# One attention-plus-FFN layer on one core: the 64-row remainders of the first FFN matrix as pairs on the two row halves, its bias in the evictions, and the first chunk's projection in six pieces

## The chip, the cores and the metric

The kernel runs on one core of a Trainium2 chip. The metric is the device time of one execution in microseconds (us). A profiled execution has a span, from its first to its last instruction, and the time of the whole execution, which is a little longer.

## What is computed

One layer over 2048 tokens of width 576, all in bf16: a memory-augmented attention with 32 heads of 18, and a dense FFN of width 4608. `B_x` is not used: the FFN's input is the attention's output.

```python
def _A_ref(x, wq, wk, wv, wo, beta):
    q, k, v = ...                       # (B, H, N=4 segments, L=512, Dh=18)
    phi = lambda t: jnp.where(t > 0, t + 1.0, jnp.exp(t))
    g = _sigmoid(beta).reshape(1, H, 1, 1)
    ...
    for s in range(N):
        logits = jnp.einsum('bhqd,bhkd->bhqk', qs, ks) * scale + mask   # causal, inside the segment
        a_dot = jnp.einsum('bhqk,bhkd->bhqd', _softmax(logits, axis=-1), vs)
        a_mem = einsum(phi(qs), M) / (einsum(phi(qs), z) + 1e-06)
        outs.append(g * a_mem + (1.0 - g) * a_dot)
        M = M + einsum(phi(ks), vs)
        z = z + sum(phi(ks))
    return o @ wo

def _B_ref(x, w1, b1, w2, b2):
    h = _gelu(jnp.einsum('bsd,df->bsf', x, w1) + b1)
    return jnp.einsum('bsf,fd->bsd', h, w2) + b2

h = x + _A_ref(_layernorm(x), A_wq, A_wk, A_wv, A_wo, A_beta)
out = h + _B_ref(_layernorm(h), B_w1, B_b1, B_w2, B_b2)
```

## The kernel before

**Tiling.** The tokens are cut into 8 chunks of 256 (`NCH`, `Q`), each of two tiles of 128 rows (`tl`). The width 576 is contracted in five steps: four of 128 rows and a remainder of 64. In the kernel before, the remainder is 65 rows (`KTAIL`): row 65 of the moving operand holds ones, and row 65 of the weights holds a bias or zeros. The helper `mm5` (lines 321 to 324) issues the four full steps on line 323 and the 65-row step on line 324.

**Streams.** TensorE's work is written as generators, one for each part:
- `stream_P(tl)`: layernorm, the transposed input (`xT`), the projection to q, k and v (three times 576 columns, for every chunk in four pieces of 432, `CH`), its evictions into `qk_pad` and `v_aug`, and the transposes of q and k into `QT` and `KT`: on TensorE for the first two chunks (`TP`), by DMA for the others.
- `stream_A`: 80 visits. A visit is 16 score matmuls on 32-row tiles (line 512), into the four PSUM banks `st4`, an exponential over all four banks on ScalarE (line 518), masks on GpSimd (line 522), and 16 matmuls with the values into the bank `ox` (line 541).
- `stream_M`: the memory's sums; `stream_B(tl)`: the output projection, the residual, the second layernorm, and the transposed FFN input `xn2T`.
- `stream_F1`: the first FFN matrix. Its weights come in 9 groups of 512 columns for every chunk (`w1g`, two buffers, and three more inside `hT` for the first chunk). A unit is two blocks of 128 hidden units by 256 tokens, into one bank: 2 x 5 matmuls, then one eviction on VectorE (line 756) into `hT`. The bias is the 65th row of the weights. For the first chunk the first five groups (`AHEAD`) are run for each 128-token tile apart (line 733). GELU runs in place on `hT` (line 764).
- `stream_F2`: the second matrix, 36 matmuls of 288 columns into one bank (line 790), and the addition of the stored `hc` (line 794).

**PSUM.** Four banks are the scores' (`st4`). Three banks, and `ox` before the first and after the last score visit, are handed out by `bank_slots`. `f_slots` is the same object as `bank_slots`.

**Order.** The kernel plans itself before it issues anything. Every operation is recorded with an engine, an estimated duration, what it reads and writes, and a due time (`SLACK` by kind). `step` walks a simulated clock: on each engine the ready operation with the earliest due time begins; on TensorE the next stream in a fixed order (FFN first or last, by `lead` and `balance`) that is ready and has a free bank. All is then issued in the planned order, so each engine's order on the chip is fixed, and only the semaphores decide when an instruction starts. Where no stream is ready in the beginning, the plan puts in dummy matmuls (line 831).

Of the kernel before, what the change touches and what calls it, by code (L numbers as in the profile page):

```python
# [16 lines left out]
def kernel(  # L17
# [31 lines left out]
    XW = 640  # L49
    CH = 432  # L50
# [7 lines left out]
    def sbuf(name, shape, dt=BF16):  # L58
# [10 lines left out]
    SLACK = dict(head=34, lnp=34, lnb=20.5, pow=-97, apply=-7, ek_k=91, relu_k=47.5, min_k=4, add_k=59, mz=27, exp=21,  # L69
                 ek=-56, relu=43, min=76, add=-35.5, hb=-169.5, gelu=-80, finish=2.5, mem=-93, sum=-137.5, out=-24.5,  # L70
                 hd=133.5, xp=-183.5, xb=-26, t_x=-46.5, t_q=-17.5, t_k=61.5, t_o=-59, t_h=77, w1=29, w2=117, hc=15.5,
                 evict=9, qk=-57.5, ot=-2, mask=32.5, lead=1.5, balance=58.5)
    ops = []
    now, dma_free, table = 0.0, 0.0, "exp"
    free_at = {"PE": 0.0, "SP": 0.0, "ACT": 0.0, "DVE": 0.0, "POOL": 0.0}
    port_until = {"DVE": 0.0, "POOL": 0.0}
    queue = {e: [] for e in free_at}
    writer, readers, known = {}, {}, {}

    class Op:  # L80
        start, end, at, apart = None, NEVER, None, False
# [6 lines left out]
        def ready(self):  # L88
            if self.at is None:
                t = latest(self.preds, self.eng)  # L90
                if t >= NEVER:
                    return NEVER
                self.at = t
            return self.at
# [29 lines left out]
    def op(eng, dur, issue, rd=(), wr=(), slack=0.0, table=None, port=None):  # L124
        o = Op(eng, dur, issue, preds_of(rd, wr), now + slack, table)
        o.port = eng == "POOL" if port is None else port
        ops.append(o)
        queue[eng].append(o)
        note(o, rd, wr)
        return o  # L130
# [8 lines left out]
    def dma(kb, issue, rd=(), wr=(), slack=0.0):  # L139
        return transfer(op("SP", 0.46, issue, rd, wr, slack), kb, 1.66, rd, wr)  # L140
# [6 lines left out]
    def begin(o):  # L147
        nonlocal dma_free, table
# [4 lines left out]
        if getattr(o, "port", False):  # L153
            dur += max(0.0, port_until["POOL" if o.eng == "DVE" else "DVE"] - now)
            port_until[o.eng] = now + dur
        if o.eng == "SP":
            dur = max(dur, dma_free - now - 6.0)
        o.start, o.end = now, now + dur
# [4 lines left out]
        elif d:  # L163
            dma_free = max(dma_free, o.end - o.dur + d.first) + d.dur / DMA_RATE
            d.start, d.end = o.start, dma_free + 0.9
        queue[o.eng].remove(o)

    class Slots:
# [13 lines left out]
        def when(self):  # L182
            return min((self.at(k) for k in self.free), default=NEVER)
# [15 lines left out]
    w1_bufs = [sbuf(f"w1g{j}", [KT, 512]) for j in range(2)]  # L199
    ident = sbuf("ident", [P])  # L200
    mhalf = sbuf("mhalf", [1], F32)
# [39 lines left out]
    LATER, AHEAD = 0, 5  # L241
    f_slots = bank_slots
# [7 lines left out]
    b1_row = B_b1.rearrange("(o f) -> o f", o=1)  # L250
# [8 lines left out]
    def memset(eng, dur, ap, value, key, slack=0.0):  # L259
        e = nc.vector if eng == "DVE" else nc.gpsimd  # L260
        op(eng, dur, lambda: e.memset(ap, value), (), [key], slack)
# [9 lines left out]
    def constants():  # L271
        op("POOL", 0.75, lambda: make_identity(nc, ident[:]), (), ["ident"])
# [11 lines left out]
        for tl in range(2):  # L284
            layernorm(f"p{tl}", x_p[tl][:], ("x_p", tl), xn1[tl], ("xn1", tl), False, -5)
# [5 lines left out]
        for j in range(2):  # L291
            memset("POOL", 0.45, phik_pads[j][:, :, Dh:32], 0.0, ("phik", j, "pad"), slack=5)
        for j in range(2):
            memset("POOL", 0.2, o_nats[j][:, :, D:XW], 0.0, ("o", j, "pad"), slack=6)
            memset("POOL", 0.15, xn2[j][:, D:XW], 0.0, ("xn2", j, "pad"), slack=6)
# [585 lines left out]
```

## Time and profile before

| | |
|---|---|
| time, median of 3 runs | 481.13 us (479.82 to 482.57) |
| the profiled execution's own time | 484.58 us |
| its span | 482.9 us |
| mean granted TensorE clock | 0.992 |
| busy share of the span: TensorE, VectorE, ScalarE, GpSimd | 98%, 58%, 60%, 43% |
| TensorE matmuls | 6084 |

In the profile, PE is TensorE's matmuls, PEld its weight loads, DVE VectorE, ACT ScalarE, POOL GpSimd, SP the engine that issues the DMAs. A matmul's shown duration reaches from its start to its modelled end; matmuls in a row overlap, so the slot that one takes is read from the starts. In a timeline row the columns are start, duration (both us), engine, line, operation, tiles, rows x columns of the array, shape, and the count of merged instructions; brackets hold the idle time before it and what ended that.

### The profile page before, as it was taken

The numbers are of one execution on the slowest core, as the hardware profiler recorded it, in microseconds if no ns is written. First come the engines' busy times: TensorE is split into PE (matmuls) and PEld (weight loads), VectorE is DVE, ScalarE is ACT, GpSimd is POOL, SyncE is SP. The second block draws the span as 40 slices with busy tenths as digits, with TensorE's granted clock in tenths as the row PEclk, the third lists the DMA queues.
The fourth block names the chain that finished last, engine by engine and source line by source line (L and its number), as shares of the span: only waits on it lengthen the run. The fifth ranks groups of instructions, "written<-read, shape, count | busy, mean of one in ns | idle before, by whom it ended". The sixth has DMA issues, their size and how long they took to land.

```text
span 482.9 us, 14420 instructions
## 1 busy us (share of the span) xinstructions
PE 471.1 (98%) x6084; PEld 369.5 (77%) x6084; DVE 282.4 (58%) x688; ACT 289.9 (60%) x206; POOL 207.2 (43%) x291
## 2 busy tenths in 40 slices
PE   7989899999999999999999999999999999999997
PEld 5667778768678878767788888778787788888875
DVE  5787776768676563667685546756555345334401
ACT  2669578971695877951687868475587762213200
POOL 5558355475736342684654343845534511000000
PEclk9989899999999999999999999999999999999999
DMA  7985679779788547668967569693667267646311
GB/s 215 293 280 187 125 128 252 162 144 177 152 169 213 172 118 205 177 121 198 214 136 190 123 165 203 158 233 104 155 196 186 78 190 195 185 124 186 97 50 50
DMA packets 117345, 80.97 MB, mean 168 GB/s; under 512 B 56392, under 2 KB 115232, under 8 KB 117280
## 3 DMA queue, kind: packets, MB, share of 16 engines
q1 hardware_dynamic: 117248, 80.04, 68.0%
q8 instruction: 48, 0.79, 0.7%
q14 instruction: 17, 0.14, 0.1%
q0 software_dynamic: 32, 0.01, 0.1%
HBM read 60.10 MB, written 7.08 MB: 139 GB/s over the span
## 4 chain that ended last, share of the span: by engine, by line
PE 89%; DMA 4%; DVE 3%; issue 1%; POOL 1%; SPq 1%; ACT 1%; DVEq 0%; POOLq 0%
PE bank L323 38%; PE bank L790 23%; PE bank L324 9%; PE ox L541 6%; PE st L512 5%; PE ox L790 4%; DMA wqkv<-in_A_wv_dram 2%; DMA w1g<-in_B_w_dram 1%; PE ox L323 1%; DMA xT<-o_nat 1%; PE bank L564 1%; PE bank L470 1%; PE bank L431 1%; DVE gmzm L311 1%; ACT pt L518 0%
## 5 line engine op out<-in xcount | busy, mean ns | idle before, releaser
L518 ACT ACTIVATE pt<-st 128x2048 bf16<-128x2048 f32 x80 | 150.2, 1877 | 67.1 <-PE st L512 63.7
L323 PE MATMUL bank<-xn2T,w1g 128*128 128x256 bf16 (+1 forms) x1064 | 147.9, 269 | 0.5 <-DVE hT L736 0.3
L790 PE MATMUL bank<-w_sb,hT 128*128 128x288 bf16 x1008 | 138.3, 286 | 0.0
L756 DVE CAST hT<-bank 128x512 bf16<-128x512 f32 x129 | 88.7, 689 | 73.6 <-PE bank L324 72.5
L790 PEld LDWEIGHTS <-hT 128*128 128x128 bf16 x1152 | 109.3, 98 | 28.0
L522 POOL TENSOR_SCALAR_AFFINE_SELECT pt<-pt 128x512 bf16<-128x512 bf16 x128 | 81.0, 648 | 101.6 <-ACT pt L518 101.1
L323 PEld LDWEIGHTS <-w1g 128*128 128x128 bf16 x1104 | 101.0, 97 | 16.8 <-DMA w1g<-in_B_w_dram 0.5
L764 ACT ACTIVATE hT<-hT 128x4608 bf16<-128x4608 bf16 (+4 forms) x23 | 66.1, 2875 | 49.5 <-DVE hT L756 49.4
L324 PE MATMUL bank<-xn2T,w1g 65*128 65x256 bf16 (+1 forms) x266 | 72.1, 271 | 0.0
L323 PE MATMUL bank<-wqkv,xT 128*128 128x432 bf16 x252 | 56.4, 346 | 0.7 <-DMA xT<-xn 0.4
L323 PEld LDWEIGHTS <-xT 128*128 128x128 bf16 x384 | 35.0, 98 | 23.5 <-issue 2.3
L541 PEld LDWEIGHTS <-pt 128*128 128x128 bf16 x1280 | 43.4, 96 | 8.2 <-issue 2.1
L541 PE MATMUL ox<-v_aug,pt 128*128 128x19 bf16 x1280 | 45.8, 172 | 2.0 <-issue 2.0
L512 PE MATMUL st<-QT,KT 32*128 32x128 bf16 x1280 | 32.4, 218 | 0.1
L556 POOL TENSOR_TENSOR pq<-ek,pq 128x512 bf16<-128x512 bf16 x24 | 27.7, 1153 | 6.9 <-DVE ek L554 6.5
L406 ACT CAST qk_pad<-bank 128x432 bf16<-128x432 f32 x31 | 15.8, 522 | 24.7 <-PE bank L324 21.8
L794 DVE TENSOR_TENSOR ot<-bank,hc 128x288 bf16<-128x288 f32 x28 | 12.7, 454 | 28.6 <-PE bank L790 28.1
L512 PEld LDWEIGHTS <-KT 32*128 32x128 bf16 x1280 | 18.7, 93 | 14.0 <-issue 11.7
L324 PEld LDWEIGHTS <-w1g 65*128 65x128 bf16 x276 | 26.8, 97 | 3.2
L586 POOL TENSOR_TENSOR o_nat<-t,t 128x288 bf16<-128x288 f32 x24 | 19.5, 811 | 12.0 <-DVE t L585 11.9
L677 POOL TENSOR_TENSOR h_t<-h_t,b_bc 128x576 f32<-128x576 f32 x16 | 20.6, 1286 | 5.6 <-DVE xn L343 5.6
L324 PE MATMUL bank<-wqkv,xT 65*128 65x432 bf16 x63 | 21.9, 348 | 0.0
(101 smaller groups left out, 484.7 us busy)
## 6 DMA issues: line engine op xcount, KB each, us to landing
w1g<-in_B_w_dram SPq DMA_DIRECT2D x67, 512.0 KB
w_sb<-in_B_w_dram SPq DMA_DIRECT2D x6, 864.0 KB
hd<-h_t SPq DMA_DIRECT2D x16, 288.0 KB
hc<-hd SPq DMA_DIRECT2D x32, 144.0 KB
w1g<-in_B_w_dram SPq DMA_DIRECT2D x67, 64.0 KB
x_b<-in_A_x_dram SPq DMA_DIRECT2D x18, 144.0 KB
hT<-in_B_w_dram SPq DMA_DIRECT2D x5, 512.0 KB
out_dram<-ot SPq DMA_DIRECT2D x16, 144.0 KB
```

Source lines behind the costliest of these rows:

```text
L323: nc.tensor.matmul(out=out_ap, lhsT=lhsT_of(slice(0, P), k), rhs=rhs_of(slice(0, P), k), start=(k == 0), stop=False)
L324: nc.tensor.matmul(out=out_ap, lhsT=lhsT_of(slice(0, KTAIL), 4), rhs=rhs_of(slice(0, KTAIL), 4), start=False, stop=True)
L512: nc.tensor.matmul(out=st4[:, i, n * P:(n + 1) * P], lhsT=KTs[(c - c % 2 + kt // 2) % 3][rows, g, (kt % 2) * P:(kt % 2 + 1) * P], rhs=QTs[ ...
L518: op("ACT", 1.88, lambda: nc.scalar.activation(out=pt[:], in_=st4[:], func=ACT.Exp, scale=scale), sk, [("pt", slot, n) for n in range(4)], ...
L522: op("POOL", 0.65, lambda n=n: nc.gpsimd.affine_select(out=pt[:, :, n * P:(n + 1) * P], in_=pt[:, :, n * P:(n + 1) * P], pattern=[[0, 4], ...
L541: nc.tensor.matmul(out=oxv[:, 4 * (g % 4) + i, :], lhsT=pts[slot][:, i, n * P:(n + 1) * P], rhs=v_augs[(2 * s0 + kt) % 6][:, 4 * g + i, :] ...
L556: op("POOL", 1.16, lambda: nc.gpsimd.tensor_tensor(out=pq[:], in0=e_g, in1=pq[:], op=ALU.add), ["ek"], ["pq"], slack=SLACK["add"])
L586: op("POOL", 0.8, lambda: nc.gpsimd.tensor_tensor(out=o_dst, in0=t1[:], in1=t2[:], op=ALU.add), ["t1", "t2"], ok, slack=SLACK["sum"])
L677: op("POOL", 1.36, lambda: nc.gpsimd.tensor_tensor(out=h_t[:], in0=h_t[:], in1=b2_bc[:], op=ALU.add), ["b2"], [("h", tl)], slack=SLACK["hb"])
L756: op("DVE", 0.684, lambda hT=hT, jp=jp, acc=acc: nc.vector.tensor_copy(out=hT[:, 2 * jp:2 * jp + 2, :], in_=acc), [b], [("hT", c % 2, jp)] ...
L764: op("ACT", (f1 - f0) * Q * 0.00083 + 0.18, lambda hT=hT, f0=f0, f1=f1: nc.scalar.activation(out=hT[:, f0:f1, :], in_=hT[:, f0:f1, :], fun ...
L790: nc.tensor.matmul(out=acc, lhsT=hT[:, q, tl * P:(tl + 1) * P], rhs=w2_sb[:, q, hs], start=(q == 0), stop=(q == NF - 1))
```

## The change

**Remainders.** From the sixth group of the first chunk on, a weight group's bank pair is opened by four 64-row matmuls, two on the upper and two on the lower row half of the array, and the sixteen full steps follow. For this the remainder of the weights is stored as 64 rows by 256 columns on partitions 0 to 63 and again 256 columns on partitions 64 to 127, and `xn2` is written with its last 64 columns twice, so that its transpose has the remainder on both row halves. A group takes two banks at once. For the first five groups of the first chunk the remainder runs as a full step of 128 rows against `xz`, which is zero on the other half.

**Bias.** `b1` is loaded once as 36 rows, transposed on TensorE into `b1T`, and added in the eviction: on VectorE as an addition with a broadcast operand, or on ScalarE as two activations with a bias. The planner takes the engine that is free first (`either`); the same choice is given to the copies of the projection and of the transposes.

**First chunk.** Its projection is cut in six pieces of 288 columns (`NS`); the transposes of q and of k follow directly on their two pieces, and the scores may start before v is projected (`half_V`).

**Planner.** It knows a cost for a change of the tiling (`SWITCH`), chooses the order of remainders and scores by it, models TensorE's code fetch and the port that VectorE and GpSimd share otherwise, holds GpSimd's early memsets by `hold`, and has other durations and other values of `SLACK`. The scores' four banks are used by the scores alone, as before; `f_slots` is gone.

```diff
+    W1 = 4 * 512 + 256
...
-    SLACK = dict(head=34, lnp=34, lnb=20.5, pow=-97, apply=-7, ...
+    SLACK = dict(head=61, lnp=21.5, lnb=50, pow=-21, apply=-5.5, ...
+                 out=-29.5, ..., alone=-163, linger=128.6,
+                 x1=151.5, hold=-1, ln0=86.5)
...
+    def either(first, second, rd, wr, slack=0.0):
+        o = op(*first, rd, wr, slack)
+        o.ways = {eng: (dur, issue) for eng, dur, issue in (first, second)}
+        queue[second[0]].append(o)
+        return o
...
+        if o.eng == "PE" and o.mode != tiling:
+            dur += SWITCH
+            tiling = o.mode
...
-    f_slots = bank_slots
...
     for tl in range(2):
-        load_x(2 + tl, x_b[tl], ("x_b", tl))
+        load_x(2 + tl, x_b[tl], ("x_b", tl), SLACK["x1"])
...
+        memset("POOL", 0.3, xz[:], 0.0, "xz0", slack=6, hold=SLACK["hold"])
...
+        def apply():
+            for to, f0, f1 in ((0, 0, D), (D, 512, D))[0:2 if f32 else 1]:
+                nc.vector.tensor_scalar(out=dst[:, to:to + f1 - f0], in0=src[:, f0:f1], scalar1=mv[:, 0:1], scalar2=rstd[:],
+                                        op0=ALU.subtract, op1=ALU.mult)
...
+            cuts = [(n, n + HALF) for n in range(0, 3 * D, HALF)] if c < NS else [(n, n + CH) for n in range(0, 3 * D, CH)]
...
+            def move(dst, src, n, key):
+                either(("ACT", n * 0.00083 + 0.16, lambda: nc.scalar.copy(out=dst, in_=src)),
+                       ("DVE", n * 0.00104 + 0.16, lambda: nc.vector.tensor_copy(out=dst, in_=src)), [b], [key])
...
+                    yield need(lambda: all(kt in half_V for kt in key_tiles(c, {kt for _, kt in units})), None,
+                               [("pt", slot, n) for n in part] + value_keys(c, units), ["ox"])
...
-        dma(64, lambda: nc.sync.dma_start(out=wt[0:64, 4, :], in_=B_w1[512:576, fcols]), (), [k + ("t",)], SLACK["w1"])
-        dma(1, lambda: nc.sync.dma_start(out=wt[64:KTAIL, 4, :], in_=b1_row[:, fcols]), (), [k + ("b",)], SLACK["w1"])
+        for h in range(2):
+            f0 = fg * 512 + h * Q
+            dma(45, lambda h=h, f0=f0: nc.sync.dma_start(out=wt[64 * h:64 * h + 64, 4 * 512:W1], in_=B_w1[512:576, f0:f0 + Q]),
+                (), [(*k, h)], SLACK["w1"])
...
+        op("PE", 0.06, lambda pt=pt: nc.tensor.transpose(out=pt, in_=b1_rows[:], identity=ident[:]), ["b1r", "ident"], [b])
+        op("DVE", 0.15, lambda pt=pt: nc.vector.tensor_copy(out=b1T[:], in_=pt[:, 0:NF]), [b], ["b1T"])
...
-                    op("PE", 5 * mm(Q), lambda acc=acc, a=a, fs=fs, wt=wt, c=c: mm5(
-                        acc[:, a, :], lambda r, k: wt[r, k, fs], lambda r, k: xn2T[c % 4][r, k, :]), xk + wk, [b])
-                op("DVE", 0.684, lambda hT=hT, jp=jp, acc=acc: nc.vector.tensor_copy(out=hT[:, 2 * jp:2 * jp + 2, :], in_=acc),
-                   [b], [("hT", c % 2, jp)], slack=SLACK["evict"])
+                yield need(lambda: c in done_B and (c < 2 or c - 2 in done_F2), bank_slots, xk + wk, mode=64, n=2)
+                bs = [bank_slots.take() for _ in range(2)]
+                accs = [banks[b][:].rearrange("p (a w) -> p a w", w=Q) for b in bs]
+
+                def tails(accs=accs, wt=wt, c=c):
+                    for a in range(2):
+                        for h in range(2):
+                            rows = slice(64 * h, 64 * h + 64)
+                            nc.tensor.matmul(out=accs[h][:, a, :], lhsT=wt[rows, 4 * 512 + a * P:4 * 512 + (a + 1) * P], rhs=xn2T[c % 4][rows, 4, :],
+                                             start=(a == 0), stop=False, skip_group_check=True)
+
+                op("PE", 2 * mm(Q), tails, xk + wk, bs, n=8, mode=64)
+                for h in range(2):
...
+                            for k in range(4):
+                                nc.tensor.matmul(out=acc[:, a, :], lhsT=w1_main(wt)[:, k, (2 * h + a) * P:(2 * h + a + 1) * P], rhs=xn2T[c % 4][:, k, :],
+                                                 start=False, stop=(k == 3), skip_group_check=True)
...
+                    either(("DVE", 0.69, lambda hT=hT, f=f, acc=acc: nc.vector.tensor_tensor(
+                        out=hT[:, f:f + 2, :], in0=acc, in1=bias(f, 2, Q), op=ALU.add)), ("ACT", 0.84, add),
+                        [b, "b1T"], [("hT", c % 2, f // 2)], slack=SLACK["evict"])
...
+            opens = F1 in can and waits[F1].mode == 64
+            score = scorer in can and waits[scorer].mode == 32
...
+            if score and tiling == 64:
+                can = [scorer]
+            elif opens and score and (can[0] is scorer or can[0] is F1):
+                can = [F1]
+            elif opens and not score and len(can) > 1 and now - opened[0] < SLACK["alone"]:
+                can.remove(F1)
+            elif score and len(can) > 1 and now < waits[F1]() < now + SLACK["linger"] and waits[F1].mode == 64:
+                can.remove(scorer)
```

More of the change, by code (lines that the diff above doesn't have):

```diff
@@ L820, in step @@
         ffn = [F2, F1] if work["F2"] + SLACK["balance"] <= work["F1"] else [F1, F2]
[L821 to L826 removed]
+        order = ffn + first if len(done_B) - work["F1"] / 18 > SLACK["lead"] else first + ffn
+        for g in order:
+            if g in waits and not waits[g].idle and waits[g]() <= now:
+                go_on(g)
+                return True
+        if free_at["PE"] <= now:
+            can = [g for g in order if g in waits and waits[g].idle and waits[g]() <= now]
+            opens = F1 in can and waits[F1].mode == 64
+            score = scorer in can and waits[scorer].mode == 32
+            if opens and not opened[0]:
+                opened[0] = now
+            if score and tiling == 64:
[6 more added lines that the diff above has]
+                can.remove(scorer)
+            if can:
+                if can[0] is F1 and opens:
+                    opened[0] = 0.0
+                go_on(can[0])
                 return True
```

360 lines of the change are left out of this document (210 added, 150 removed).

## The prediction

> **What bounds the kernel now.** The page first: how busy is each engine, and when.
>
> ```profile
> span 482.9 us, 14420 instructions
> ...
> PE 471.1 (98%) x6084; PEld 369.5 (77%) x6084; DVE 282.4 (58%) x688; ACT 289.9 (60%) x206; POOL 207.2 (43%) x291
> ```
>
> TensorE (PE) is at 98%, no other engine over 60%. An average can hide stages, so the windows come next.
>
> ```profile
> 0.00:20.00 20.00, 16.84 (x138) 11.09 (x139) 11.24 (x40) 7.36 (x11) 10.18 (x25) 1.00 0.90 251
> 20.00:40.00 20.00, 18.29 (x295) 12.78 (x293) 16.75 (x42) 14.82 (x15) 13.80 (x22) 0.91 0.72 225
> 40.00:80.00 40.00, 37.66 (x758) 30.30 (x756) 27.90 (x71) 29.31 (x24) 21.51 (x29) 0.96 0.86 181
> 120.00:389.00 269.00, 268.60 (x3669) 210.21 (x3668) 164.67 (x405) 191.10 (x126) 135.50 (x182) 1.00 0.70 167
> ```
>
> The columns are stretch, length, busy time of PE, weight loads, DVE, ACT and POOL, granted clock, DMA share, GB/s. From 120 to 389 us PE is idle for 0.4 us of 269, at full clock. So there time can only be won by taking slots out of PE's stream, and lost by making PE wait. Up to 80 us it has some 7 us of holes, and some clock withheld. Who made the holes:
>
> ```profile
> PE ox L541 <- issue: 2.0, 1, 2.0
> PE bank L350 <- DVE v_aug L411: 1.5, 1, 1.5
> PE ox L323 <- DMA wqkv<-in_A_wk_dram: 1.4, 1, 1.4
> PE bank L831 <- DVE pq L273: 1.3, 1, 1.3
> PE bank L564 <- ACT qk_pad L406: 0.5, 1, 0.5
> ...
> PE bank L323 <- DVE hT L736: 0.3, 1, 0.3
> ```
>
> That is nearly all that PE waits for; of evictions it waits for two alone, 0.8 us. So I work in two parts: the slots in the middle, and the holes of the head.
>
> **Slots: the remainders.** The timeline of PE, four groups of five in a row (starts in the first column):
>
> ```profile
> 152.40 0.60 PE L323 MATMUL bank<-xn2T,w1g 128*128 128x256 bf16 x4
> 152.83 0.27 PE L324 MATMUL bank<-xn2T,w1g 65*128 65x256 bf16 x1
> ...
> 154.48 0.27 PE L324 MATMUL bank<-xn2T,w1g 65*128 65x256 bf16 x1
> 154.59 0.65 PE L790 MATMUL bank<-w_sb,hT 128*128 128x288 bf16 x4
> ```
>
> From 152.40 to 154.59 stand four groups, 2.19 us, 0.548 each; the first four steps take 0.43 to 0.44, the 65-row step 0.11 to 0.12: it costs a full slot, 0.113 us. The change covers 72 - 5 = 67 weight groups with four such steps each, 268. They go: 268 x 0.113 = 30.3 us. In their place come 134 pairs.
>
> What a pair and a change of tiling cost has no row for 64 rows; the scores, on 32-row tiles, are nearest:
>
> ```profile
> 284.37 0.27 PE L324 MATMUL bank<-xn2T,w1g 65*128 65x256 bf16 x1
> 284.58 0.40 PE L512 MATMUL st<-QT,KT 32*128 32x128 bf16 x16
> 284.92 0.61 PE L323 MATMUL bank<-xn2T,w1g 128*128 128x256 bf16 x4
> 285.36 0.27 PE L324 MATMUL bank<-xn2T,w1g 65*128 65x256 bf16 x1
> ```
>
> The 65-row step before the scores holds 0.21 us instead of 0.113: 0.097 to go in. Then 16 matmuls of 128 columns take 0.34. One after the other they would need 16 x 0.056 (half of 0.113) = 0.9; as four at a time 0.225, which leaves 0.115 for coming out and for starting each tile. So tiles on different rows do run at once, each in its bank, and a change costs about 0.1. I take a pair at one slot, 0.113 (bounds: 0.11, and 0.226 if the halves ran in turn), and a change at 0.095, since the 0.115 holds the tiles' own starts (bounds 0.08 to 0.115).
>
> How many changes there are, the instruction order of the built program tells: 160 before (80 visits, in and out), 273 after; 19 of the 67 groups of remainders are followed directly by scores and two follow scores, and these share a change. So:
>
> - removed: 30.3
> - added: 134 x 0.113 = 15.1, and 113 x 0.095 = 10.7
> - net: -4.5 us. With a change at 0.115 it is -2.2.
>
> On row against rule: by the Trainium skill (TensorEngine Tiling (Array Packing), Key Properties) a change of tiling mode drains TensorE; it gives no time. The trace agrees, with the 0.1 us above, and this rule takes 10.7 of the 15.2 us back.
>
> The other edits on PE: six pieces of 288 instead of four of 432 stream the same 1728 columns; one transpose for `b1` (0.06); the first five groups keep a full slot for the remainder. Together 0.1 us. The scores' banks change nothing.
>
> **Evictions and banks.** Costs from the groups of lines:
>
> ```profile
> L756 DVE CAST hT<-bank 128x512 bf16<-128x512 f32 x129 | 88.7, 689 | 73.6 <-PE bank L324 72.5
> L794 DVE TENSOR_TENSOR ot<-bank,hc 128x288 bf16<-128x288 f32 x28 | 12.7, 454 | 28.6 <-PE bank L790 28.1
> L409 DVE CAST qk_pad<-bank 128x288 bf16<-128x288 f32 x16 | 7.3, 458 | 18.1 <-PE bank L324 16.8 <-ACT qk_pad L406 1.0 <-issue 0.3
> L406 ACT CAST qk_pad<-bank 128x432 bf16<-128x432 f32 x31 | 15.8, 522 | 24.7 <-PE bank L324 21.8 <-DVE KT L434 1.4 <-DVE ot L794 0.9
> L388 ACT COPY xT<-bank 128x640 bf16<-128x640 bf16 x4 | 2.8, 692 | 7.1 <-PE bank L350 7.1
> L518 ACT ACTIVATE pt<-st 128x2048 bf16<-128x2048 f32 x80 | 150.2, 1877 | 67.1 <-PE st L512 63.7
> ```
>
> On DVE an addition of 288 columns (454 ns) costs what a cast of 288 does (458), so the bias is free there: 0.69 us for 512. On ACT, 432 to 640 columns go from 522 to 692 ns, 0.82 ns each; 256 columns come to 378 ns, the two activations to 0.76 us (bounds 0.69, and 1.04 for two of 522). The order shows 56 such activations, 28 banks: ACT's 290 us become 311 of about 476, still two thirds. Behind each on ACT's queue stand the exponentials, which feed masks and values; PE has FFN work beside them.
>
> The new wait is for banks. While scores run there are three, and a weight group now opens only when two are free, so the F2 block or a projection has one. Every wait at the opening holds all of PE, since its order is fixed. Along PE's order I counted, with the slots above, the time between the last matmul into a bank and the first of its next use (between 60 and 400 us of work): under 1.6 us it was in 27 of 232 uses, and is in 79 of 239; under 1.3 in 9, now 20. A reuse needs the matmul's shown 0.27, the eviction's 0.69 and the signals, some 1.1 us. So before, the holes stayed near zero with 9 close cases; now some of the 20 will wait for 0.1 to 0.3 us. I take +1.5 us; bounds 0, and 79 x 0.13 = 10 (a rival below).
>
> **The head.** PE there, with the first projection, the first scores and the stall:
>
> ```profile
> 6.76 0.45 PE L350 MATMUL bank<-ident,xn 128*128 128x128 bf16 x5 [0.20 <-DVE xn L343]
> ...
> 8.00 0.90 PE L323 MATMUL bank<-wqkv,xT 128*128 128x432 bf16 x4
> ...
> 10.50 0.89 PE L323 MATMUL ox<-wqkv,xT 128*128 128x432 bf16 x4 [1.41 <-DMA wqkv<-in_A_wk_dram]
> ...
> 12.70 0.89 PE L323 MATMUL bank<-wqkv,xT 128*128 128x432 bf16 x4 [0.30 <-DMA wqkv<-in_A_wv_dram]
> ...
> 17.35 0.40 PE L512 MATMUL st<-QT,KT 32*128 32x128 bf16 x16
> ...
> 55.53 0.23 PE L541 MATMUL ox<-v_aug,pt 128*128 128x19 bf16 x2 [1.96 <-issue]
> ```
>
> The second piece of 432 columns reaches from q into k, so PE stood until wk had come. After, four pieces of 288 need wq alone: 4 x 5 x 0.1225 = 2.45 us (154.59 is the start of four 288-column slots, 0.49). But 52 dummies stand ahead of the transposes instead of 34 (which ended at 6.76 - 0.20 = 6.56): 18 x 0.11 later, 8.5. The layernorm is not sooner, since its two powers are moved behind all of GpSimd's memsets:
>
> ```profile
> 5.08 0.57 POOL L340 TENSOR_TENSOR rstd_p<-rstd_p,mhalf 128x1 f32<-128x1 f32 x1
> 5.61 0.30 POOL L261 MEMSET xn<- 128x64 bf16 x2
> ...
> 7.12 1.15 POOL L261 MEMSET MZ_blk<- 128x608 bf16 x2
> ```
>
> POOL was through at 8.27; without the `xn2` pads (0.30 at 5.61, as much before 5.08) and with `xz` (512 columns, by the 608 of `MZ_blk` 0.5) the powers end there again, and the second tile's rows are ready near 8.8. With transposes (10 x 0.056), a copy of 0.69 and the signals the first projection is at 9.7, not 8.0. The q pieces last to 12.15, past the 10.50 at which wk was there. Then stand five pieces (5 x 0.61) and 24 transposes (24 x 0.056): first scores at 16.6 with a signal or two 16.7, instead of 17.35; three v pieces (1.84) are still to do, eight transposes (0.45) more are done. So PE is 0.7 us behind in work and the exponentials, the chain of the first two chunks, are 0.65 ahead; the 1.5 us hole behind `v_aug` may shrink, as v's evictions no longer stand before the first scores. On SP the loads of `x_b` go behind `wo`, `b2` and `b1`: some 0.8 MB by their shapes, at the first window's 251 GB/s 3.2 us later, and only the second chunk's layernorm reads them; a weight group still takes three DMAs. I take -1 us for all of it; bounds -3, and +2 if the later start is not caught up.
>
> The clock:
>
> ```profile
> 31.51:34.92 3.41, 3.41 (x36) 2.48 (x34) 1.59 (x4) 1.76 (x1) 1.22 (x2) 0.50 0.89 297
> 51.99:55.40 3.41, 1.58 (x45) 1.27 (x42) 2.36 (x5) 2.44 (x3) 2.40 (x3) 1.00 0.52 176
> 55.41:58.82 3.41, 3.29 (x43) 2.99 (x43) 1.27 (x3) 0.03 (x1) 0.74 (x2) 0.50 0.26 76
> ```
>
> After a stretch of 3.41 us in which PE was busy for 1.58, the next 3.41 run at 0.50: 1.7 us lost, twice (also after the hole before 30 us). So a hole of 2 us costs 3.7. The "issue" hole lies inside a run of 16 value matmuls, with no operand to wait for. By the Trainium skill (TensorE: Matmul & The Clock Gate, Why this matters for your kernels) idle gaps up to about 3 us cost no clock. The trace differs: here 1.96 us cost some, and the measurement decides. By the page, holes that go would give back only themselves, 3.5 us; by the rows up to 6.9. I take -1.5 for holes and clock of the stretch from 20 to 60 us, because the "issue" hole has no releaser that the change takes away.
>
> **The sum.** -4.5 (slots) + 0.1 + 1.5 (banks) - 1 - 1.5 (head) = -5.4 us. It is made on the profiled execution, 484.58 us, which lies 3.45 above the median; a hole with its cold stretch (3.7) is about that, so the timed runs may lack it. As a difference it is taken from the median: 481.13 - 5.4 = 475.7, say 476.
>
> **Rivals.**
>
> 1. *The bank pair starves PE.* A group opens only with two free banks; if an eviction stands behind an exponential (1.88 us) on ACT or another eviction on DVE, PE stands. Price: each of the 79 close reuses short by 0.13 us, 10 us: 476 - 1.5 + 10 = 484.5; it decides from 0.08 us for each of the 67 groups, which eats the whole gain. For: the doubled close cases, three banks. Against: DVE at 58% loses 28 evictions, and before, with 9 close cases, all waiting on evictions was 0.8 us. By the Trainium skill (TensorEngine Tiling, Gotcha 1) row tiling raises PSUM pressure; no row here shows it, the scores having banks of their own.
> 2. *Nothing measurable.* A change of tiling costs its upper 0.115 (-2.2) and the head gives nothing: 481.1 - 2.2 + 1.5 = 480.5. For: the first projection does start later.
> 3. *The halves overlap badly.* If the scores' 0.34 us were all streaming (0.085 for four tiles, not 0.056) and the way out still cost its 0.095, a pair would cost 0.17: 134 x 0.057 = 7.6 more, 483.6. With no overlap at all, 134 x 0.113 = 15 more, 491. Against: 0.9 us of scores in 0.34 with the way out in it. The Trainium skill (TensorE: Matmul & The Clock Gate, Measured speedup vs the span model) gives 3.07 for four row tiles; a pair at that 77% would cost 0.147 and the time be 480.5.
> 4. *The head's holes go.* All 6.9 us but the floor of -1.5 already taken: 476 - 5.4 = 470.5.
>
> **How the numbers follow.** Half a per cent, 2.4 us, is about what a measurement of this kernel can tell from no change. Forecast (473 to 479): 0.46. Rival 4 (467 to 473): 0.19. Rival 2 (479 to 482): 0.15. Rival 1 (482 to 489): 0.15. Rival 3 (481 to 491): 0.05. The range, 468 to 486, leaves out the ends of 4, 1 and 3, some 0.12. Faster by over 0.5% (under 478.7): 0.19 and 0.44 of the forecast, 0.63. Slower (over 483.5): 0.12 of rival 1 and 0.04 of rival 3, 0.16. Same: 0.21.
>
> **What would show it.** In the profile after: groups of 64-row matmuls whose second half starts some 4 ns after the first, each group with its change lasting about 0.41 us to the next full step (0.32 from remainder to scores); PE's wait list with evictions at the remainder's line under 2 us in all; wk no longer in that list; the first scores near 16.7 us; fewer than two stretches at 0.50. Wrong it would be if PE's busy share falls below 97% between 120 and 389 us, if the halves start one slot apart, or if a group costs over 0.5 us.

## The result, and the profile after

The changed kernel takes 477.04 us (476.06 to 478.30, 6 runs), the kernel before in the same job 479.85 us (479.71 to 482.57, 6 runs). The ratio of the means is 0.9929, with a 95% interval of 0.9902 to 0.9956: 3.4 us less (2.1 to 4.7). The medians differ by 2.8 us. The forecast was 476 us, 5.4 less than the median shown then. The profiled execution took 477.54 us, its span is 475.8 us, its mean granted clock 0.999.

The page of the changed kernel, the line of the busy shares:

```profile
span 475.8 us, 14492 instructions
...
PE 467.1 (98%) x6124; PEld 351.9 (74%) x6124; DVE 247.5 (52%) x640; ACT 341.6 (72%) x332; POOL 206.1 (43%) x289
```

TensorE is still the bound. VectorE has 35 us less than before, ScalarE 52 us more. The windows of the changed kernel, columns as in the prediction:

```profile
0.00:20.00 20.00, 18.68 (x194) 14.93 (x195) 9.51 (x40) 10.42 (x14) 10.07 (x23) 1.00 0.85 242
20.00:40.00 20.00, 19.89 (x348) 14.73 (x347) 16.51 (x44) 19.45 (x23) 16.77 (x25) 1.00 0.77 247
...
120.00:389.00 269.00, 267.58 (x3602) 200.48 (x3600) 143.09 (x363) 207.28 (x189) 125.96 (x169) 1.00 0.68 171
```

From 20 to 40 us PE has 0.1 us of holes, where it had 1.7, and the clock is full. In the middle it has 1.4 us of holes, where it had 0.4. Its list of waits:

```profile
PE bank L966 <- DVE pq L318: 1.2, 1, 1.2
PE bank L844 <- DVE hT L866: 1.0, 1, 1.0
PE st L570 <- ACT pt L576: 0.8, 2, 0.4
PE bank L367 <- DMA xT<-o_nat: 0.5, 1, 0.5
PE ox L599 <- DVE o_nat L641: 0.4, 1, 0.4
PE bank L844 <- DMA w1g<-in_B_w_dram: 0.4, 1, 0.4
PE bank L844 <- DVE ot L905: 0.3, 1, 0.3
```

The wait for wk, the stop with no releaser and the one behind `v_aug` are gone. New are three at L844, the 64-row remainders, 1.7 us together, and another 1.7 us elsewhere: scores behind exponentials (`pt`), matmuls behind `xT` and behind `o_nat`. The remainders in the timeline of PE, one group followed by scores and one by full steps:

```profile
283.74 0.53 PE L901 MATMUL bank<-w_sb,hT 128*128 128x288 bf16 x3
284.20 0.39 PE L844 MATMUL bank<-xn2T,w1g 64*128 64x256 bf16 x4
284.52 0.40 PE L570 MATMUL st<-QT,KT 32*128 32x128 bf16 x16
...
288.50 0.65 PE L901 MATMUL bank<-w_sb,hT 128*128 128x288 bf16 x4
289.09 0.39 PE L844 MATMUL bank<-xn2T,w1g 64*128 64x256 bf16 x4
289.41 1.05 PE L856 MATMUL bank<-xn2T,w1g 128*128 128x256 bf16 x8
```

Four F2 slots of 0.1225 end at 288.99: 0.10 to go in, then 0.32 for both pairs and the way out, 0.42 for a group. Followed by scores it is the same 0.32, but those scores pay no change of their own. Last the head, three rows of PE's timeline:

```profile
9.72 0.65 PE L367 MATMUL ox<-wqkv,xT 128*128 128x288 bf16 x4
...
12.64 0.65 PE L367 MATMUL bank<-wqkv,xT 128*128 128x288 bf16 x4
...
16.71 0.40 PE L570 MATMUL st<-QT,KT 32*128 32x128 bf16 x16
```

First projection 9.72 (forecast 9.7), first scores 16.71 (16.7), and the k piece at 12.64 waits for nothing.

### The profile page after: what moved, and what is told of

It is laid out like the page before. It is cut to its first block, busy times and chain, and to the rows that moved or that the text cites. A ratio compares the mean times of both kernels' runs of the same rounds, so it can differ in the third digit from the quotient of the medians.

```text
span 475.8 us, 14492 instructions
## 1 busy us (share of the span) xinstructions
PE 467.1 (98%) x6124; PEld 351.9 (74%) x6124; DVE 247.5 (52%) x640; ACT 341.6 (72%) x332; POOL 206.1 (43%) x289
## 4 chain that ended last, share of the span: by engine, by line
PE 87%; DMA 3%; DVE 3%; POOL 2%; SPq 2%; ACT 2%; issue 1%; POOLq 0%
PE bank L901 26%; PE bank L856 23%; PE bank L367 12%; PE ox L599 6%; PE st L570 5%; PE bank L844 4%; PE bank L368 3%; PE ox L901 3%; DMA xT<-o_nat 1%; PE bank L820 1%; ACT pt L576 1%; DMA w1g<-in_B_w_dram 1%; DMA x_p<-in_A_x_dram 1%; PE ox L856 1%; PE bank L622 1%
## 5 line engine op out<-in xcount | busy, mean ns | idle before, releaser
L901 PE MATMUL bank<-w_sb,hT 128*128 128x288 bf16 x1044 | 142.9, 286 | 0.0
L856 PE MATMUL bank<-xn2T,w1g 128*128 128x256 bf16 x1008 | 126.2, 273 | 0.0
L856 PEld LDWEIGHTS <-w1g 128*128 128x128 bf16 x1040 | 94.3, 97 | 21.1 <-issue 9.5
L866 DVE TENSOR_TENSOR hT<-bank,b1T 128x512 bf16<-128x512 f32 x77 | 52.8, 689 | 88.2 <-PE bank L856 88.0
L864 ACT ACTIVATE hT<-bank,b1T 128x256 bf16<-128x256 f32 x106 | 44.5, 471 | 40.7 <-PE bank L856 40.3
L875 ACT ACTIVATE hT<-hT 128x4608 bf16<-128x4608 bf16 (+3 forms) x22 | 65.8, 2996 | 0.4
L367 PE MATMUL bank<-wqkv,xT 128*128 128x432 bf16 (+1 forms) x264 | 56.5, 337 | 0.0
L844 PE MATMUL bank<-xn2T,w1g 64*128 64x256 bf16 x252 | 26.3, 274 | 0.8 <-DMA w1g<-in_B_w_dram 0.4
L385 POOL TENSOR_TENSOR rstd_b<-rstd_b,mhalf 128x1 f32<-128x1 f32 x16 | 8.9, 555 | 33.6 <-DVE rstd_b L380 33.6
L368 PE MATMUL bank<-wqkv,xT 65*128 65x432 bf16 (+1 forms) x66 | 22.3, 338 | 0.0
```

What stands on the lines that cost most here:

```text
L367: nc.tensor.matmul(out=out_ap, lhsT=lhsT_of(slice(0, P), k), rhs=rhs_of(slice(0, P), k), start=(k == 0), stop=False)
L368: nc.tensor.matmul(out=out_ap, lhsT=lhsT_of(slice(0, KTAIL), 4), rhs=rhs_of(slice(0, KTAIL), 4), start=False, stop=True)
L844: nc.tensor.matmul(out=accs[h][:, a, :], lhsT=wt[rows, 4 * 512 + a * P:4 * 512 + (a + 1) * P], rhs=xn2T[c % 4][rows, 4, :], start=(a == 0) ...
L856: nc.tensor.matmul(out=acc[:, a, :], lhsT=w1_main(wt)[:, k, (2 * h + a) * P:(2 * h + a + 1) * P], rhs=xn2T[c % 4][:, k, :], start=False, s ...
L864: nc.scalar.activation(out=hT[:, f + a, :], in_=acc[:, a, :], func=ACT.Identity, bias=b1T[:, f + a:f + a + 1])
L866: either(("DVE", 0.69, lambda hT=hT, f=f, acc=acc: nc.vector.tensor_tensor(out=hT[:, f:f + 2, :], in0=acc, in1=bias(f, 2, Q), op=ALU.add)) ...
```

## Experiments

### The kernel before, once more

No edit. The profile in the prediction had two stretches at half clock; is that the usual run?

> The kernel before once more, with a new profile. Theory: the 1.96 us stop inside a run of 16 value matmuls at 53.6 us and the half-clock stretch behind it belong to that one profiled execution; this one has neither, its span is 478 to 479 us and its time about 479.8, so that some 3.7 us of the difference between the two profiles are not the change's. Rival: the stop is there again, within a microsecond of the same place.

480.29 us, span 478.6, clock 0.999. Its list of waits and one row of its windows:

```profile
PE bank L350 <- DVE v_aug L411: 1.5, 1, 1.5
...
PE ox L323 <- DMA wqkv<-in_A_wk_dram: 1.2, 1, 1.2
PE ox L541 <- issue: 0.7, 1, 0.7
```

```profile
120.00:389.00 269.00, 268.95 (x3692) 211.70 (x3691) 163.76 (x402) 191.99 (x125) 134.02 (x180) 1.00 0.66 168
```

The holes are there. The "issue" stop is back inside the same run of 16 value matmuls, at 53.4 us, but 0.7 us long instead of 2.0, and no stretch of the head is at half clock: the theory holds for the clock, and for the stop only in part. The timed runs of the experiments list a granted clock. Of 58 runs of the kernel before in their four jobs, 34 have 0.999 or 1.0 and a median of 479.85 us; 24 have 0.992 to 0.996 and a median of 481.98. One stretch of 3.41 us at half clock loses 1.7 us, 0.36% of the span, which fits 0.996; two make 0.993. (That the runs without a profile have such a stretch, and where, isn't shown.) The 12 runs of the changed kernel all have 0.999 or 1.0, median 477.1. So at equal clock the change brings 2.75 us, and 24/58 x 2.1 = 0.9 us on average is clock that only the kernel before loses. This profile, not the prediction's, is the one to set beside that of the changed kernel: 480.29 against 477.54, the same 2.75. (In part by chance: the 12 runs of the changed kernel alone spread over 2.3 us.)

### Do the two halves overlap?

```diff
-                            rows = slice(64 * h, 64 * h + 64)
+                            rows = slice(0, 64)
```

> The changed kernel with all four 64-row matmuls of a group on the upper row half (the second block then takes the weights and inputs of the first: that part of the result is another). Number and order of the instructions and of the tiling changes stay. Theory (the halves overlap): each second matmul of a pair waits a full slot of 0.107 to 0.113 us, 134 times: +14.3 to +15.1 us on the changed kernel, 491 to 492. Rival (the halves hardly overlap, or PE has room): under +4 us.

490.04 us against 480.45, 1.0195 (1.0154 to 1.0235): 12.8 us on the changed kernel, somewhat under the 14.3 to 15.1 expected. PE's timeline of this kernel, a group followed by scores:

```profile
286.43 0.61 PE L844 MATMUL bank<-xn2T,w1g 64*128 64x256 bf16 x4
286.97 0.40 PE L570 MATMUL st<-QT,KT 32*128 32x128 bf16 x16
```

On one half, four matmuls take 0.54 us instead of 0.32, two slots more. 67 x 0.22 = 14.7. The difference to 12.8 is in the waits: in its list L844 keeps 0.3 us on evictions and none on weights, as everything else has more time. So a pair is one slot, and the rival with badly overlapping halves is out.

### What do the pairs bring beside full steps?

```diff
-                            rows = slice(64 * h, 64 * h + 64)
+                            rows = slice(0, P)
```

> The changed kernel with the four remainders of a group as matmuls over all 128 rows, one after the other, and so without a change of tiling (both halves' products are summed, the result is another). Planned order, banks and evictions stay. Theory: 268 slots of 0.109 = 29.2 us instead of 67 x (0.230 + 0.010) = 16.1 us for pairs and 113 changes x 0.0935 = 10.6: +2.5 us on the changed kernel, 479.5, that is the pairs alone bring about 2.5 us. Rival 1 (the pairs bring all of the gain): +3.4 or more. Rival 2 (the pairs bring nothing, the gain is the head's and the plan's): 0 or below.

479.25 us against 480.45, 0.9988 (0.9967 to 1.0009). On the changed kernel that is 2.2 us by the medians and 2.8 by the ratios. Two groups in its timeline of PE, one before scores and one before full steps:

```profile
285.48 0.60 PE L844 MATMUL bank<-xn2T,w1g 128*128 128x256 bf16 x4
286.01 0.40 PE L570 MATMUL st<-QT,KT 32*128 32x128 bf16 x16
...
290.47 0.60 PE L844 MATMUL bank<-xn2T,w1g 128*128 128x256 bf16 x4
290.91 1.04 PE L856 MATMUL bank<-xn2T,w1g 128*128 128x256 bf16 x8
```

Before full steps four full slots take 0.44 us, the pairs with both changes 0.42, and the full step behind the pairs is 0.01 longer: next to nothing. Before scores it is 0.53 against 0.10 + 0.32 = 0.42. By these rows 21 groups beside scores bring 21 x 0.11 = 2.3 us and the other 46 some 0.5: by this sum, most of what the pairs bring comes from sharing a change with the scores. (The sum agrees with the times; the two kinds of group were not run apart. The spans of the two profiled executions differ by 1.4 us only, since this one has 1.6 us fewer waits behind 80 us.) The rest of the slots' gain is the 65-row step itself, 0.114 us by its starts in the kernel before, against 0.109 for a full one: 268 x 0.005 = 1.3 us.

### What does a change of tiling cost?

The second pair of each group is issued four steps later, so that every group opens the 64-row tiling twice.

```diff
+                            if h == 0 and a == 1:
+                                tails(only=1)
```

> The changed kernel with the second pair of each group issued four full steps later, so that each of the 67 groups has two more changes of tiling and nothing else. Theory (a change costs 0.095 us wherever it stands): 67 x 2 x 0.095 = +12.7 us, less where the first change was shared with scores (19 groups keep theirs): 12 to 13 us, 489 to 490. Rival (a change is partly hidden by weights loaded ahead, and the scores' 0.34 us overstate it): +4 to +8.

489.77 us, 1.0196 (1.0160 to 1.0231): 12.8 us for 134 changes more, 0.095 each by the time, the value taken. That is rough: in the profiled executions the spans differ by 11.0 us, and the stops behind 80 us are 1.1 us here instead of 4.2. The rows of its timeline of PE give the price itself:

```profile
285.85 0.60 PE L858 MATMUL bank<-xn2T,w1g 128*128 128x256 bf16 x4
286.38 0.28 PE L844 MATMUL bank<-xn2T,w1g 64*128 64x256 bf16 x2
286.59 1.49 PE L858 MATMUL bank<-xn2T,w1g 128*128 128x256 bf16 x12
```

Four slots of 0.109 end at 286.29: 0.09 in, and 0.21 for a pair of 0.115 and the way out, so 0.095 out.

### The changed kernel again, and in four pieces

> The changed kernel once more, beside the kernel before and the three that follow, on the same chip. Theory and rival alike: 0.993 of the kernel before. It is there to be compared with.

477.09 us against 480.92, 0.9918 (0.9895 to 0.9941), span 474.7. Beside it, with the due times of the plan set anew:

```diff
-    LATER, AHEAD, NS = 0, 5, 1
+    LATER, AHEAD, NS = 0, 5, 0
...
-                op("PE", 2 * mm(Q), tails, xk + wk, bs, n=8, mode=64)
+                op("PE", 2 * mm(Q) + 0.027, tails, xk + wk, bs, n=8, mode=64)
```

> The changed kernel with the first chunk's projection in four pieces of 432 (NS = 0), as before; its due times were searched anew for this, since the old ones make a bad plan with it, and its plan knows the measured cost of a pair. Remainders, bias and evictions stay. Theory (the six pieces and the early scores give the 2.3 us of the head that the two kernels' profiles differ by): +1.5 to +2.5 us on the changed kernel, first scores at 17 us or later. Rival (the head's gain is the planner's, not the pieces'): within 1 us of the changed kernel.

480.51 us against the same 480.92, 0.9991 (0.9968 to 1.0014): 3.4 us on the changed kernel, over the 1.5 to 2.5 expected. First scores at 18.46 instead of 16.71. Its windows:

```profile
0.00:20.00 20.00, 18.34 (x158) 12.77 (x159) 9.85 (x38) 8.21 (x13) 9.81 (x22) 1.00 0.91 253
20.00:40.00 20.00, 18.82 (x322) 13.38 (x323) 16.75 (x46) 18.29 (x21) 16.07 (x26) 1.00 0.64 189
...
120.00:389.00 269.00, 266.69 (x3668) 200.03 (x3661) 147.55 (x374) 208.45 (x181) 128.16 (x174) 1.00 0.69 169
```

Up to 40 us PE has 2.8 us of holes, in the changed kernel 1.4: that is the head, 1.4 us, near the 1.75 of the scores. In the useful matmuls done by 65 us, counted at their slots, it is about 1.8 us behind. In the middle it has 0.9 us more; its list names 1.5 us for weight groups at L845. The due times are others too, so neither part can be put down to the pieces alone; by the head, six pieces with their plan are worth about 1.5 us.

### Is ScalarE's share of the evictions needed?

All evictions of the first FFN matrix on VectorE, the due times set anew, the same estimate of a remainder:

```diff
-                    either(("DVE", 0.69, ... ), ("ACT", 0.84, add),
+                    op("DVE", 0.69, ...
```

> The changed kernel with every eviction of the first FFN matrix on VectorE, none on ScalarE; due times searched anew, and the plan knows the measured cost of a pair. VectorE takes 56 more additions of 0.69 us (247 to 286 us busy), ScalarE loses 112 activations (342 to about 295). Theory (DVE was far from full, ScalarE's share is not needed): within 1 us of the changed kernel, or faster by up to 1.5. Rival (two banks must be emptied at once, one engine is too slow for it): +3 us or more, with PE's waits for hT evictions on DVE over 3 us.

478.43 us, 0.9945 (0.9915 to 0.9975), 1.3 us on the changed kernel, with intervals that overlap. Its list of waits:

```profile
PE bank L845 <- DMA w1g<-in_B_w_dram: 2.6, 4, 1.6
PE bank L845 <- DVE hT L867: 1.3, 2, 1.1
```

Waiting for evictions is about where it was; what is longer are the waits for weights. The due times are others here too, so what brings them isn't shown. The 3 us of the rival did not come, and the 1.3 us lie within the noise: the second engine for evictions is worth little.

### Is the head bound by the two powers on GpSimd?

The powers of the first layernorm come ahead in GpSimd's order, with 18 dummies left out; then ahead of all its early memsets, with 23 left out.

```diff
+        early = [o for o in ops if o.eng == "POOL" and o.dur == 0.56 and o.start < 9.0]
+        for o in early:
+            o.start = max(q.start for q in o.preds if q.eng == "DVE") + 0.001
```

> The changed kernel with the first layernorm's two powers on GpSimd as soon as their input is there, ahead of the later memsets, and with 34 dummies instead of 52 ahead of the first transposes; all else in the planned order. wq's bytes are there at 5.5 us, wk's at 8.5, wv's at 10.5. Theory (the first projection was held by the powers behind the memsets, at 9.72 us): it starts near 8.1, the first scores near 15.1 instead of 16.7, and as PE is the bound all that follows is 1.6 us earlier: -1.6 us. Rival (something else in the head ends last, wk or the chain of the exponentials): the gain is lost by 40 us, -0.5 us or nothing.

477.11 us, 0.9924 (0.9898 to 0.9950): no change, but the premise wasn't reached. First projection 9.64. VectorE's timeline, then GpSimd's:

```profile
5.83 0.51 DVE L389 TENSOR_SCALAR xn<-x_p,mv_p,rstd_p 128x576 bf16<-128x576 bf16 x1
7.52 1.22 DVE L389 TENSOR_SCALAR xn<-x_p,mv_p,rstd_p 128x576 bf16<-128x576 bf16 x1 [1.19 <-POOL rstd_p L385]
```

```profile
6.93 0.56 POOL L385 TENSOR_TENSOR rstd_p<-rstd_p,mhalf 128x1 f32<-128x1 f32 x1
7.43 1.15 POOL L305 MEMSET MZ_blk<- 128x608 bf16 x2
```

The second power still stood behind memsets, and the second tile's normalization took 1.22 us beside the memset of `MZ_blk`, against 0.51 for the first.

> The changed kernel with both powers of the first layernorm ahead of all of GpSimd's later memsets and with 34 dummies, none between the transposes and the first projection; all else in the planned order. In e8 only the first power was early: the second stood behind wo's memset, and the second tile's rows came at 8.8 us as before. In e5, whose plan has both powers first, the first scores came at 14.85 us. Theory (PE is the bound, so a head that is over sooner moves all that follows): first projection by 8.3, first scores near 15.2 instead of 16.7, and -1.3 to -1.5 us at the end. Rival (from 20 to 80 us the chain through exponentials, masks and layernorm, or DMA, ends last): the lead is gone by the 16th visit, at the end within 0.5 us of the changed kernel.

475.85 us against 481.07, 0.9898 (0.9873 to 0.9923). Now first projection 8.14 and first scores 15.15, 1.56 us sooner than in the changed kernel. The fifth visit's scores in the timelines of PE, of this kernel and of the changed one run again:

```profile
28.44 0.40 PE L570 MATMUL st<-QT,KT 32*128 32x128 bf16 x16
```

```profile
28.63 0.40 PE L570 MATMUL st<-QT,KT 32*128 32x128 bf16 x16
```

0.19 us is left of the lead, and as much at the 16th visit (61.04 us against 61.23): that far the rival is right. Where the lead went stands in VectorE's timeline, then PE's:

```profile
16.02 0.46 DVE L375 BATCH_NORM_STATS2 stats_p<-x_b 128x6 f32<-128x288 bf16 x1 [1.92 <-DMA x_b<-in_A_x_dram]
16.40 0.81 DVE L448 CAST v_aug<-bank 128x288 bf16<-128x288 f32 x2
```

```profile
16.89 0.22 PE L792 MATMUL bank<-ident,b_rows 128*128 128x128 bf16 x1 [0.62 <-DVE v_aug L448]
```

VectorE stands 1.92 us for a tile of the second chunk's input (in the changed kernel run again 0.21), two evictions of v stand behind it, and PE waits for them. The transfer lands near 16 us in both kernels, and behind it 0.47 us of the lead is left (the transposes at L486 start at 17.91 us against 18.38). In its fixed order PE still runs the 18 dummies that the changed kernel has between 17 and 22 us.

This kernel has the best ratio of all. Whether it is faster isn't settled: its median is 1.2 us under that of the changed kernel, more than the rival's 0.5, but it ran in another job, the intervals overlap, and the profiled spans are alike (474.6 us, and 474.7 for the changed kernel run again).

### A plan that knows the waits

A pair is planned 0.027 us longer, weights come slower (250 for 270, landing 0.3 to 0.4 us later), the stall of code fetches is halved, and the due times are set anew.

```diff
-    DMA_RATE = 270.0
+    DMA_RATE = 250.0
```

> The changed kernel planned anew with what the runs measured: a pair group's true cost (0.027 us more), code fetch half as dear, transfers slower (250 instead of 270 and 0.3 to 0.4 us more to land), and due times searched for that; both powers come first in this plan. The program's parts are the same, 277 changes of tiling. Theory (2.8 of the changed kernel's microseconds are waits that its plan did not see, for evictions behind a late x tile and for weight groups): PE's waits after 80 us under 1.5 us instead of 4, and 1 to 3 us faster than the changed kernel, 0.986 to 0.991 of the kernel before. Rival (a plan made for slow transfers gives up as much as it saves): within 1 us of the changed kernel.

477.15 us, 0.9924 (0.9896 to 0.9953), as the changed kernel. Its window of the middle:

```profile
120.00:389.00 269.00, 269.00 (x3682) 200.74 (x3683) 148.80 (x381) 211.84 (x186) 132.68 (x179) 1.00 0.72 171
```

No hole is left there, and no wait stands at the remainders in its list. Counted from the starts, its stops behind 80 us come to 2.2 us; the changed kernel has 4.2 and, run again, about 2.8. So the theory's 1.5 us was missed, and the time is the rival's. Four changes of tiling more take 0.4 us back; the rest isn't found. It is not in the head: the 17th visit's scores start at 66.08 us, in the changed kernel at 65.14, but in another order, and the useful matmuls done by 65 us are as many.

### The stop at 82 us

In the changed kernel PE's longest stop behind the head stands at a remainder. PE's timeline, then VectorE's:

```profile
82.39 0.28 PE L844 MATMUL bank<-xn2T,hT 64*128 64x256 bf16 x1
83.62 0.38 PE L844 MATMUL bank<-xn2T,hT 64*128 64x256 bf16 x3 [0.96 <-DVE hT L866]
```

```profile
81.72 0.82 DVE L375 BATCH_NORM_STATS2 stats_p<-x_p 128x6 f32<-128x288 bf16 x2 [1.23 <-DMA x_p<-in_A_x_dram]
...
82.89 1.28 DVE L866 TENSOR_TENSOR hT<-bank,b1T 128x512 bf16<-128x512 f32 x2
```

VectorE stood for 1.23 us at the head of its queue, waiting for a tile of x; two finished banks waited behind it, and PE for them. The experiment takes the kernel with the powers first and puts the two evictions ahead of that layernorm.

```diff
+        rest = max(o.start for o in (ops[601], ops[604]))
+        for n in range(4):
+            ops[569 + n].start = rest + 0.001 * (n + 1)
```

> The kernel of e8b with one more change of order: on VectorE the two evictions at 82 us go ahead of the layernorm statistics that wait for an x tile (BNStats, aggregate and the power behind them), instead of behind. In the changed kernel PE stood at 82.4 us for 1.2 to 1.45 us at a pair's second matmul, whose bank those evictions had to empty, while VectorE stood 1.2 to 1.5 us for the tile. Theory (the wait for two banks is a wait for what stands ahead of the evictions): that stop goes below 0.2 us, the 24th visit's scores start 1.0 to 1.3 us earlier than in e8b (107.6), and the end is 1 us earlier. Rival (the lead is taken back by the layernorm that is now later, or by the next weight group): the 36th visit within 0.3 us of e8b's 166.2, the time the same.

477.19 us against 481.85, 0.9919 (0.9890 to 0.9949). In its timelines of PE and GpSimd:

```profile
81.64 0.39 PE L844 MATMUL bank<-xn2T,hT 64*128 64x256 bf16 x4
...
84.69 0.26 PE L599 MATMUL ox<-v_aug,pt 128*128 128x19 bf16 x4 [1.59 <-POOL pt L580]
```

```profile
83.49 0.55 POOL L385 TENSOR_TENSOR rstd_p<-rstd_p,mhalf 128x1 f32<-128x1 f32 x1 [2.17 <-DVE rstd_p L380]
84.00 0.63 POOL L580 TENSOR_SCALAR_AFFINE_SELECT pt<-pt 128x512 bf16<-128x512 bf16 x1
```

The stop at the remainders is gone and stands at the values: the layernorm ended later, so its power on GpSimd did, and a mask stood behind that. The visit's scores that the kernel with the powers first has at 107.62 us start at 108.14, 0.5 us later instead of 1.0 to 1.3 earlier. Three of its six runs have a clock of 0.996 and a median of 477.76, three have 1.0 and 476.41. So this order has lost again what it gained at the remainders, and in half of its runs some clock as well.

## Why the prediction was right, and where not

The forecast was faster by 5.4 us; by the ratios it is 3.4 and 3.9 us in the two jobs. By its steps:

1. **Slots: -4.5 forecast, -3.9 found.** The mechanism stands, by the runs on one half and with two openings. A change was taken at 0.095 and is 0.095. The terms that were off are the pair and what follows it: a pair comes to 0.115 (0.42 for a lone group, less two changes, for two pairs), and the first full step behind a group takes 0.119 instead of 0.109. With 16.1 for 134 pairs and 10.6 for the changes, against 30.55 for the removed steps, -3.9 is left. A lone group is 0.42 to 0.43 us where about 0.41 was named, and it is 0.32 to the scores, as named. The second half starts 3 to 4 ns after the first by the trace. The Trainium skill (TensorE: Matmul & The Clock Gate, Measured speedup vs the span model) puts about 4 ns for each tile, which the trace shows; the 77% that the prediction took from its 3.07 for four tiles doesn't hold for two halves here, 0.115 being hardly over a slot.

2. **Banks: +1.5 forecast, +2.8 found for all waits.** Counted from the starts (a stop shows as idle only beyond the 0.16 us of the last matmul's tail), PE stops behind 80 us for 1.4 us in the kernel before (its second profile) and for 4.2 after. By cause the 4.2 are 2.4 for banks, 1.1 for weight groups and 0.7 for the transposed attention output; the changed kernel run again has about 2.8, of which 2.1 for banks. The bound 0 to 10 held, and the rival of 10 us did not come. What failed is the reason for the size: the close reuses of banks were taken at 0.1 to 0.3 us each. Instead most fit, and a few long stops make up the sum, one of 1.2 where VectorE's queue stood behind a transfer. The waits for weights had been put at nothing. A plan with slower transfers and longer pairs took the middle's holes away and no time off the whole.

3. **ScalarE.** The prediction read 56 rows of activations as 28 banks. Each row stood for two, so it is 56 banks:

```profile
L866 DVE TENSOR_TENSOR hT<-bank,b1T 128x512 bf16<-128x512 f32 x77 | 52.8, 689 | 88.2 <-PE bank L856 88.0
L864 ACT ACTIVATE hT<-bank,b1T 128x256 bf16<-128x256 f32 x106 | 44.5, 471 | 40.7 <-PE bank L856 40.3
```

(Six more read `ox` and stand in a group of their own, 112 in all.) One takes 471 ns, not the 378 by the line through two copies, so ScalarE has 341.6 us instead of 311. No wait in PE's list is for one of them, so no cost of it is seen. On VectorE the addition takes 689 ns, exactly the cast's time: the bias is free there, as said.

4. **Head: -1 and -1.5 forecast.** First projection and first scores came at the forecast times. At the 17th visit's scores the changed kernel (65.14 us) is 1.2 us ahead of the profile of before at full clock (66.38), and with the useful matmuls that it has done more by then about 2.3. The sum of 2.5 was right, its make-up not, so that it came out is in part luck: in the profile quoted, 3.4 us lay in cold stretches, of which the usual run has none. The later loads of `x_b`, too, had been priced for the second chunk's layernorm alone; with an earlier head, as the run with the powers first shows, v's evictions stand behind them.

5. **Clock.** The prediction left open whether the timed runs lack the cold stretch. Four in ten of the kernel before list a lower clock, and no run of the changed kernel does. On the gaps, the Trainium skill (TensorE: Matmul & The Clock Gate, Why this matters for your kernels) lets up to about 3 us pass at no cost in clock. The first profile differs, with its cold stretch behind a hole of 1.96 us. The runs without a profile fit that but don't show it: the kernel before, with holes of 1.2 to 1.5 us, loses clock in 24 of 58, and the kernel with a new stop of 1.59 us in 3 of 6. The second profile has the 1.5 us hole at full clock, and the four-piece kernel, with no wait over 1.2 us in its list, loses clock in 2 of 12. The measurement decides: shorter gaps can cost clock; which of them do stays open.

At equal clock the ledger is -3.9 (slots) + 0.1 + 2.8 (waits) - 2.3 (head) = -3.3, against 2.75 measured; 0.5 us is not accounted for. With 0.9 for the clock the average is 3.65, between the two ratios. The forecast missed by some 1.5 to 2 us, of which 1.3 is the waits and 0.6 the slots. Of the rivals, the one with badly overlapping halves is refuted, the starving banks came at 2.4 us of their 10, and "nothing measurable" and "all holes go" lie outside the interval. No run has the program of before with newly searched due times, so what the planner brings by itself, in the head above all, isn't shown apart.

No kernel run here is clearly faster than the changed one. Each removed hole showed the next: the earlier head ends at a transfer that VectorE waits for, the freed evictions move a stop to a mask.

## What to carry to other kernels

A packed matmul pays if its change of tiling is shared: here a lone pair group saved 0.01 us over full steps and one beside the scores 0.11, so first place such groups next to others that already change tiling. On a kernel with 98% on one engine in a fixed order, cost the added waits by what can stand at the head of each queue (a layernorm waiting for a transfer, here at 16 and at 82 us), not by the mean time of a reuse. And see a second profile before a hole or a cold stretch is booked as a gain; it may be that of some runs only.

## What the runs showed of the hardware

- A 65-row step costs 0.114 us between starts, a 128-row step of 256 columns 0.109, and the first full step behind 64-row tiles 0.119, as behind the scores' 32-row tiles.
- A change of tiling costs 0.09 to 0.10 us: into 64-row tiles, out of them, and into the scores' 32-row tiles from 64 rows as from 65. (The way out of the scores was not told apart from the tiles' own starts.)
- VectorE's normalization of 128 x 576 takes longer beside GpSimd. In the 13 traces, none of the 117 with no GpSimd instruction beside them takes over 0.58 us (0.42 from bf16, 0.57 from float32). The 299 with one take 0.41 to 1.48 us, half of them over 0.8, as the 1.22 us beside the memset of `MZ_blk`. Which instructions of GpSimd do it was not tried apart.
- An activation with a bias over 256 columns takes 0.471 us on ScalarE, while 432 columns are copied in 0.52.
- In the first profile a stretch of 3.41 us at half clock loses 1.7 us. The 24 of 58 runs of that program that list a clock of 0.992 to 0.996 have a median 2.1 us longer than the others (481.98 against 479.85).
